# Column-tiled attention outputs, a new plan and another hand-over in a three-stage kernel

## The chip, the cores and the metric

One core of one Trainium2 chip runs the whole program; there is no communication. The metric is the device time of one execution in microseconds (us). Engines are named as the profile names them: PE is TensorE (PEld its weight loads), DVE is VectorE, ACT is ScalarE, POOL is GpSimd, SP is SyncE, whose queue issues nearly all DMAs. Each engine works through its own instructions in order, and waits on the others by semaphores.

## The reference

Three layers, one after the other, all in float32. `layout` lays the inputs out on the host before the kernel is launched, as it did before.

```python
# 1. attention with a complex decay: B, H, S, D = 2, 8, 768, 48
scale = np.minimum(mag, 0.999) / (mag + 1e-06)        # mag = |a_re + i a_im|
for t in range(S):
    S_re, S_im = a*S (complex) + k[t] v[t]^T           # state: D x D per head
    y[:, :, t] = q[t] @ S_re
# 2. mixture of experts on the 1536 x 384 rows: E = 8, F = 1024, capacity 384
e = argmax(x @ w_gate); pos = running count of e       # each row goes to one expert
y = relu(disp[e] @ w1[e]) @ w2[e];  out[i] = gate[i] * y[e, pos]
# 3. feed-forward, d_ff = 2048
h = x @ w_in
out = (max(h, 0) + alpha * min(h, 0)) @ w_out
```

## The kernel before

**Attention and routing.** The 2 x 768 positions are 12 tiles of 128 (tiles 0 to 5 are the first batch, 6 to 11 the second). The recurrence is done by chunks: for each tile `log_polar` and `turns` take logarithm and angle of the decay, `decay` and `turns` sum them along the tile by a product with a triangular matrix (`pl`, `pt`), `rotate` scales and turns k and q (`kk`, `qq`, 96 numbers a head: cosine and sine parts), and `attend` does the rest. In `attend`, per half of four heads: `tr` transposes kk and qq by PE (`pkT`, `pqT`) and evicts them to `kT`, `qT`; `scores` makes the 128 x 128 products `sc` and masks them to `pT`; `outs` adds `pT` times v and `qT` times the carried state `Z` into `y`; `state` makes the tile's addition `u` to the state. Two DVE operations then update `Z`. In `outs` (L614, L618) the stationary operand is `pT` or `qT` of a head, and 128 columns of v or Z stream through, 48 of which are the head's; the 80 others fall on columns that the next head's product writes again. `y` so has positions on partitions and heads along the row, and is copied to `x`.

`route` takes groups of tiles: it transposes `x` (`px`), evicts `xT`, multiplies with the gate weights (`lg`), picks the expert, counts positions, and POOL scatters the rows of `x` to a buffer `xs_d` in HBM by an indirect DMA. That buffer, and parts of `ys_d` and `gs_d`, are cleared first by `clear` from a zeroed tile.

The order of all this is made by `Plan`: every step is entered with an engine, a cost and a rank, and `order` lists them by a greedy simulation; `emit` then ties the instructions of each engine in that order. Tables at the top of the file (GROUPS, RANK, SQUARE, EVICT, TURN) say how tiles are grouped for the two activation tables, which step goes first, and which engine takes the squares of `log_polar`, the evictions of `kT` and `qT`, and the rounding in `turns`. `whole` and `preload` load the first experts' weights during attention: float32 weights are split into a high part `wh` (ACT) and a low part `wl` (DVE) of type fp32r (L889, L893).

**Experts.** `first_expert` builds the input of expert 0 without waiting for the last scatter. `ffn` then runs 8 experts over 256 rows: per step `ft` nine products into `hp` (three weight/input pairs for each of three 128-row blocks), ACT and DVE make `gh` and `gl`, and `second` adds six products into two `y` tiles. Hooks in each step convert the next weights (`unit`, L288 to L294), gather the next expert's rows and transpose them (`split_rows`). `first_chunk` prepares the input of the third layer; it reads the scattered gates back from `gs_d` into `gsl`, and `first_chunk_rows` adds the rows of other experts.

**Feed-forward.** `ffn` three times over 512 rows and 16 steps; at each end four `y` tiles are evicted to `o` and stored.

Of the kernel before, what the change touches and what calls it, by code (L numbers as in the profile page):

```python
# [21 lines left out]
P = 128  # L22
HD = 48
NH = 8
DM = NH * HD
VW = DM - HD + P
# [11 lines left out]
C_TRI, C_TRIP, C_ONE, C_LAST, C_STRI, C_COL = (i * P for i in range(6))  # L38
C_IOT = C_COL + 2
C_TWIN = C_IOT + GT * NE  # L40
GROUPS = [[0], [1], [2, 3], [4, 5], [6, 7], [8, 9], [10, 11]]
# [6 lines left out]
SQUARE = 'AAAAAAAAAAAA'  # L48
EVICT = 'AAAA'
DOUBLE = (('AAA', 'GGG'),) * NTL  # L50
TURN = 'AV' * 6
ABS = 'V' * NTL
C_ACT, C_BIAS, C_TT, C_STT, C_PS, C_WIDE, C_SQ = 0.415, 0.51, 0.47, 0.5, 0.47, 0.87, 0.79
# [3 lines left out]
RANK = {'L': -4.0, 'T': -3.5, 'D': -2.0, 'R': -1.5, 'E': -0.5, 'A': 0.0, 'O': 0.5}  # L57
# [8 lines left out]
HK1 = 9  # L66


class Plan:
# [9 lines left out]
    def op(self, engine, cost, fn, use=(), put=(), new=(), after=(), lag=None, port=False):  # L79
# [19 lines left out]
        self.ops.append(dict(engine=engine, cost=cost, fn=fn, deps=deps, new=list(new), lag=lag, rank=self.rank, port=port))  # L99
        return n  # L100

    def order(self):
# [9 lines left out]
        start, done = [None] * n, [None] * n  # L112
        free = {}
# [9 lines left out]
        while ready:  # L123
            best = []
            for i in ready:
# [17 lines left out]
                ((t, i) for t, i in best if ops[i]["engine"] == engine and t <= first + SLACK), key=lambda x: (-ops[x[1]]["rank"], rest[x[1]], -x[1])  # L143
            )
            o = ops[i]
            start[i] = t
            done[i] = t + o["cost"] + o["lag"]
            free[o["engine"]] = t + o["cost"]
            if o["port"]:
                free["port"] = t + o["cost"]  # L150
# [20 lines left out]
def const_array():  # L171
# [5 lines left out]
    for c in range(2):  # L177
# [6 lines left out]
        [tri, tri / (2 * math.pi), one, last, tri - np.eye(P), cq, ck, io, twin, np.eye(P), np.tile(np.arange(SLOTS), (P, 1))],  # L184
# [6 lines left out]
def tile_kernel(  # L191
# [114 lines left out]
    wg = acp.tile([P, KC, NE], F32, name="wg")  # L306
# [20 lines left out]
    for t in vt:  # L327
        G.memset(t[:, DM:VW], 0.0)
    Zt = [acp.tile([96, VW], F32, name=f"Z{i}") for i in range(B)]
    for t in Zt:  # L330
        G.memset(t[:, DM:VW], 0.0)
        G.memset(t[:, 0:DM], 0.0)
# [34 lines left out]
    def load(g, names, cost=0.6):  # L367
        for i in groups[g]:
            for nm in names:
                src = {"ar": a_re, "ai": a_im, "q": q, "k": k, "v": v}[nm]  # L370

                def fn(i=i, nm=nm, src=src):
                    if nm == "v":
                        dst = tl[f"v{i}"] = vt[i % 6]
                        dst = dst[:, 0:DM]
                    else:
                        dst = buf(raw, nm, f"{nm}{i}", [P, DM], RAW[nm])
# [59 lines left out]
    def decay(i):  # L437
# [3 lines left out]
        def pl():  # L441
# [3 lines left out]
               use=[f"l{i}", "cst"], put=[p], new=[("pc", p)])  # L445
# [114 lines left out]
    def attend(i):  # L560
# [6 lines left out]
        def y():  # L567
            return psum("y", f"y{i}", [P, 512])
# [726 lines left out]
```

## Time and profile before

| | |
|---|---|
| median of 3 runs | 561.19 us (559.08 to 561.61) |
| the profiled execution | 555.74 us, of which the span of its instructions 554.0 us |
| mean granted TensorE clock | 0.983 |
| busy: PE, PEld | 508.6 us (92%), 466.2 us (84%) |
| busy: DVE, ACT, POOL | 336.1 us (61%), 321.6 us (58%), 71.7 us (13%) |
| DMA | 71.04 MB, mean 128 GB/s |

The profile is of one execution. Busy times are shares of the whole span, over stages that have different limits, so they have to be taken stage by stage. From 0 to about 182 us the core does attention and routing, to about 343 us the eight experts, to about 546 us the feed-forward layer; the rest is the last store. A matmul of float32 operands appears as two instructions (two passes), one of fp32r operands as one.

### The profile page before, as it was taken

The page shows a single profiled execution, that of the slowest core. Times are in us where ns is not written, and L with a number is a line of the kernel's source. Part 1 is how long each engine was busy: PE and PEld are TensorE (multiplying, and loading weights), DVE is VectorE, ACT ScalarE, POOL GpSimd, SP SyncE. Part 2 cuts the span into 40 slices and gives each one's busy share as a digit, 9 for nine tenths or more (in the row PEclk, how much of TensorE's full clock was granted, in tenths as well). Part 3 has the DMA queues.
Part 4 walks back from the last instruction along what each step waited for, and adds up shares of the span by engine and source line. Part 5 has one row for each costly group of instructions (what it writes and reads, how often), then busy time and mean ns, then how long its engine had stood idle before and what let it go on. Part 6 is the DMA issues. An engine that isn't in the chain of part 4 may idle for free.

```text
span 554.0 us, 8596 instructions
## 1 busy us (share of the span) xinstructions
PE 508.6 (92%) x3270; PEld 466.2 (84%) x3270; DVE 336.1 (61%) x617; ACT 321.6 (58%) x601; POOL 71.7 (13%) x83
## 2 busy tenths in 40 slices
PE   1677999999998969999999998999999999999994
PEld 0466798888997958999999986988999989999993
DVE  2555889997663536676658969797933433333431
ACT  6589999995643346665656425464644534443432
POOL 2203126160512400000000020202000000000000
PEclk9978999999999989999999999999999999999998
DMA  8897534320001557788886466354101000100001
GB/s 270 291 397 253 147 101 157 116 87 0 30 12 47 114 173 246 230 249 264 268 304 188 143 200 205 105 160 135 54 0 58 1 0 1 43 15 1 1 0 63
DMA packets 37411, 71.04 MB, mean 128 GB/s; under 512 B 4105, under 2 KB 30098, under 8 KB 36594
## 3 DMA queue, kind: packets, MB, share of 16 engines
q1 hardware_dynamic: 35570, 65.30, 36.5%
q0 software_dynamic: 1792, 5.12, 2.8%
q8 instruction: 27, 0.44, 0.4%
q14 instruction: 22, 0.18, 0.1%
HBM read 55.84 MB, written 14.56 MB: 127 GB/s over the span
## 4 chain that ended last, share of the span: by engine, by line
PE 71%; DVE 10%; DMA 8%; ACT 6%; issue 2%; POOL 1%; SPq 0%; POOLq 0%; DVEq 0%; ACTq 0%
PE hp L1033 26%; PE y L1023 26%; PE y L614 3%; PE sc L599 3%; PE y L618 2%; PE u L631 2%; DMA gs_d<-gate,sidx 2%; PE pqT L580 1%; DMA sw<-in_moe_w_out 1%; DMA st<-in_moe_w 1%; DVE wl L294 1%; PE pt L492 1%; PE pt L1005 1%; DMA cst<-in_consts 1%; PE pkT L580 1%
## 5 line engine op out<-in xcount | busy, mean ns | idle before, releaser
L1023 PE MATMUL y<-wh,gh 128*128 128x384 f32 x320 | 109.6, 343 | 3.8 <-ACT gh L1041 3.8
L1033 PE MATMUL hp<-xl,wh 128*128 128x256 f32 (+1 forms) x336 | 111.0, 330 | 2.1 <-DVE xl L1008 1.0
L1033 PE MATMUL hp<-xh,wh 128*128 128x256 f32 (+1 forms) x336 | 111.5, 332 | 1.2 <-ACT xh L1007 1.0
L1033 PE MATMUL hp<-xh,wl 128*128 128x256 f32 (+1 forms) x336 | 110.8, 330 | 0.0
L1023 PE MATMUL y<-wl,gh 128*128 128x384 f32 x320 | 108.0, 337 | 0.0
L1023 PE MATMUL y<-wh,gl 128*128 128x384 f32 x320 | 89.3, 339 | 0.3 <-DVE gl L1042 0.2
L294 DVE TENSOR_TENSOR wl<-st,wh 128x768 fp32r<-128x768 f32 (+1 forms) x63 | 67.5, 1071 | 32.8 <-ACT wh L293 31.6
L293 ACT ACTIVATE wh<-st 128x768 fp32r<-128x768 f32 (+1 forms) x63 | 59.0, 936 | 28.8 <-DMA st<-in_moe_w 20.6
L1048 DVE SCALAR_TENSOR_TENSOR gn<-gn,nalp,gp 128x512 f32<-128x512 f32 x48 | 36.0, 749 | 62.5 <-ACT gp L1047 62.5
L1046 ACT ACTIVATE gn<-hp 128x512 f32<-128x512 f32 x48 | 28.7, 598 | 71.2 <-PE hp L1033 60.4
L1033 PEld LDWEIGHTS hp<-xl,wh 128*128 128x128 f32 x336 | 63.5, 189 | 7.6 <-DVE xl L1008 1.2
L1033 PEld LDWEIGHTS hp<-xh,wh 128*128 128x128 f32 x336 | 63.5, 189 | 7.1 <-ACT xh L1007 1.3
L1033 PEld LDWEIGHTS hp<-xh,wl 128*128 128x128 f32 x336 | 63.6, 189 | 5.0
L1023 PEld LDWEIGHTS y<-wh,gh 128*128 128x128 f32 x320 | 60.4, 189 | 5.6 <-ACT gh L1041 4.2
L1023 PEld LDWEIGHTS y<-wl,gh 128*128 128x128 f32 x320 | 60.6, 189 | 1.3
L1023 PEld LDWEIGHTS y<-wh,gl 128*128 128x128 f32 x320 | 57.0, 189 | 1.4 <-DVE gl L1042 0.9
L1050 DVE TENSOR_TENSOR gl<-gn,gh 128x512 fp32r<-128x512 f32 x48 | 33.2, 691 | 29.5 <-ACT gh L1049 29.5
L1041 ACT ACTIVATE gh<-hp 128x256 fp32r<-128x256 f32 x64 | 24.5, 383 | 44.0 <-PE hp L1033 39.6
L390 POOL TENSOR_TENSOR ai<-ai 128x384 f32<-128x384 f32 x36 | 34.9, 969 | 75.7 <-ACT ai L447 73.8
L1049 ACT ACTIVATE gh<-gn 128x512 fp32r<-128x512 f32 x48 | 30.2, 629 | 22.0 <-DVE gn L1048 21.9
L614 PE MATMUL y<-vt,pT 128*128 128x128 f32 x192 | 36.8, 284 | 2.3 <-DVE pT L605 2.2
L1042 DVE SCALAR_TENSOR_TENSOR gl<-hp,gh 128x256 fp32r<-128x256 f32 x64 | 26.7, 421 | 12.0 <-ACT gh L1041 11.8
(166 smaller groups left out, 810.8 us busy)
## 6 DMA issues: line engine op xcount, KB each, us to landing
st<-in_moe_w SPq DMA_DIRECT2D x24, 512.0 KB, 4.5
st<-in_moe_w SPq DMA_DIRECT2D x32, 384.0 KB, 3.9
sw<-in_moe_w_in SPq DMA_DIRECT2D x6, 1024.0 KB, 5.0
sw<-in_moe_w_out SPq DMA_DIRECT2D x8, 768.0 KB, 4.3
xs_d<-zero SPq DMA_DIRECT2D x1, 4608.0 KB, 15.6
ys_d<-o SPq DMA_DIRECT2D x16, 192.0 KB, 4.0
rows<-xs_d SPq DMA_DIRECT2D x14, 192.0 KB, 4.7
ar<-in_a_re SPq DMA_DIRECT2D x12, 192.0 KB, 3.5
```

What stands on the lines that cost most here:

```text
L293: follow(A(out=wh[:, js], in_=st, func=ACTF.Copy), behind, "A")
L294: ins = eng[j].tensor_tensor(out=wl[:, js], in0=st, in1=wh[:, js].bitcast(F32), op=ALU.subtract)
L390: (V if e == "V" else G).tensor_tensor(out=t, in0=t, in1=t, op=ALU.mult)
L614: T.matmul(out=y()[:, o:o + P], lhsT=tl[f"pT{i}{hh}"][:, h, :], rhs=tl[vk][:, o:o + P], start=True, stop=(c == 0))
L1023: T.matmul(out=ys[t], lhsT=a[:, sl], rhs=b[:, f, :], start=(ft == 0 and m == 0), stop=(ft == nf - 1 and m == 2))
L1033: ins = T.matmul(out=hp, lhsT=a[:, c, fs], rhs=b[:, c, :], start=(n == 0), stop=(n == 3 * KC - 1))
L1041: last["A"] = A(out=gh, in_=hp, func=ACTF.Relu)
L1042: last["V"] = V.scalar_tensor_tensor(out=gl, in0=hp, scalar=0.0, in1=gh.bitcast(F32), op0=ALU.max, op1=ALU.subtract)
L1046: A(out=gn, in_=hp, func=ACTF.Relu, scale=-1.0)
L1048: V.scalar_tensor_tensor(out=gn, in0=gn, scalar=nalp[:, ft:ft + 1], in1=gp, op0=ALU.mult, op1=ALU.add)
L1049: last["A"] = A(out=gh, in_=gn, func=ACTF.Copy)
L1050: last["V"] = V.tensor_tensor(out=gl, in0=gn, in1=gh.bitcast(F32), op=ALU.subtract)
```

## The change

`outs` swaps its operands: v and Z (padded to 64 columns a head, HW = 64) are stationary, 64 columns wide, and `pT` or `qT` streams through. The output of a head is transposed, 64 partitions by 128 positions, and two heads share a 128-partition block of `y`, one in the lower and one in the upper 64 columns of the array. `y` is then already what `route` needs as `xT` (with padded gate weights, four blocks of 128 in place of three); `back` and `rows` turn it back to rows `x` for the scatter. `state` streams 64 columns in place of 96. There is one `Z` for both batches, and the first tile's update is one operation.

The plan gets other groups and ranks; the squares of `log_polar`, all roundings of `turns` and one of four evictions move to DVE; `setup` gets a late rank; `xs_d` is cleared in four pieces later on, `ys_d` and `gs_d` after the first routing. `keep_warm` puts products without use (13 in all) ahead of products for which the plan sees a gap. In the experts, `behind_weights` puts gathers and the load of `gsl` behind the weight loads on SP, step 0 takes the low-part inputs last, half of `first_chunk_rows` moves to the last step, and the last evictions of the feed-forward layer alternate between DVE and ACT with four buffers.

```diff
+HW = 64
-VW = DM - HD + P
+VW = NH * HW
-GROUPS = [[0], [1], [2, 3], [4, 5], [6, 7], [8, 9], [10, 11]]
+GROUPS = [[0], [1, 2], [3, 4], [5, 6], [7, 8], [9, 10], [11]]
-SQUARE = 'AAAAAAAAAAAA'
-EVICT = 'AAAA'
-TURN = 'AV' * 6
+SQUARE = 'V' * NTL
+EVICT = 'AAAV'
+TURN = 'V' * NTL
-RANK = {'L': -4.0, 'T': -3.5, 'D': -2.0, 'R': -1.5, 'E': -0.5, 'A': 0.0, 'O': 0.5}
+RANK = {'L': -6, 'T': -2.5, 'D': -2.2, 'R': -1.3, 'E': -2.1, 'A': -0.3, 'O': 1}
...
         def outs(hh):
             def products():
-                for h in range(4):
-                    o = (4 * hh + h) * HD
-                    T.matmul(
-                        out=y()[:, o:o + P], lhsT=tl[f"pT{i}{hh}"][:, h, :], rhs=tl[vk][:, o:o + P], start=True, stop=(c == 0)
-                    )
-                    if c:
-                        T.matmul(
-                            out=y()[:, o:o + P], lhsT=tl[f"qT{i}{hh}"][:, h, :], rhs=Z[:, o:o + P], start=False, stop=True
-                        )
+                for j in range(2):
+                    for w, (src, dst) in enumerate(((tl[vk], f"pT{i}{hh}"), (Z, f"qT{i}{hh}"))[:2 if c else 1]):
+                        for m in range(2):
+                            h = 2 * j + m
+                            o = (4 * hh + h) * HW
+                            T.matmul(
+                                out=y()[m * HW:(m + 1) * HW, 2 * hh + j, :], lhsT=src[:, o:o + HW], rhs=tl[dst][:, h, :],
+                                start=(w == 0), stop=(w == 1 or c == 0),
+                            )
...
         def out():
-            xt[i] = xpool.tile([P, DM], F32, tag="x", name="x", bufs=6)
-            A(out=xt[i], in_=y()[:, 0:DM], func=ACTF.Copy)
+            A(out=buf(wk, "xT", xk, [P, H // 2, P], GT), in_=y(), func=ACTF.Copy)
+        def back():
+            pt = psum("tr", p, [P, H // 2, P])
+            for j in range(H // 2):
+                T.transpose(pt[:, j, :], tl[xk][:, j, :], ident)
+        def rows():
...
-            plan.op("S", 18.0, clear, use=["ar6", "k4"], put=["zeroed"], lag=2.2)
+        if g in CLEAR:
+            plan.rank = CLEAR_RANK
+            for n in range(4):
+                plan.op("S", 3.6, lambda n=n: clear(n), use=[CLEAR[g]], put=["zeroed"], lag=2.2)
...
+    def keep_warm(where, n):
+        for _ in range(n):
+            T.matmul(out=where(), lhsT=tri[:, 0:where().shape[0]], rhs=tri, start=True, stop=True)
...
-            for c in range(KC):
-                for a, b in ((uh, xh), (uh, xl), (ul, xh)):
+            terms = ((uh, xh), (ul, xh), (uh, xl))
+            if ft:
+                order = [(c, a, b) for c in range(KC) for a, b in terms]
+            else:
+                order = [(c, a, b) for c in range(KC) for a, b in terms[:2]] + [(c, *terms[2]) for c in range(KC)]
...
-            o = fp.tile([P, DM], F32, tag="o", name="o", bufs=3)
-            A(out=o, in_=ys[t], func=ACTF.Copy)
+            last_ones = len(ends) > 1
+            o = fp.tile([P, DM], F32, tag="rows" if last_ones else "o", name="o", bufs=4 if last_ones else OB)
+            if ends[t % len(ends)] == "A":
+                A(out=o, in_=ys[t], func=ACTF.Copy)
+            else:
+                V.tensor_copy(out=o, in_=ys[t])
...
+    def behind_weights(ins):
+        tc.add_manual_dep(ins.ins, wloads[max(wloads)].ins.name, NOSYNC, reason="weights are needed sooner")
...
+        if e == NE - 1:
+            hooks[FT - 1].append(lambda behind: first_chunk_rows(behind, range(CHT // 2, CHT)))
```

What the plan makes of it shows in the order of the engines' instructions. On PE, before, the outputs of tile 1 (`y`, from the second tile's `pT` and `qT`) stand after its first scores; the next rows repeat the last two for the other heads:

```order
L599 MATMUL sc_514<-qT_508,kT_442 128x128 x4
L580 MATMUL pqT_523<-ident,qq_409 96x128 x4
L690 MATMUL px_535<-ident,x 128x128 x3
L614 MATMUL y_543<-vt_114,pT_530 128x128
L618 MATMUL y_543<-Z_125,qT_508 128x128
```

The same place in the change, tile 1 again (`px` is now the turning back of the transposed output):

```order
L607 MATMUL sc_545<-qT_538,kT_520 128x128 x4
L587 MATMUL pkT_556<-ident,kk_502 96x128 x4
L626 MATMUL y_564<-pT_553,vt_114 64x128 x2
L626 MATMUL y_564<-qT_515,Z 64x128 x2
L626 MATMUL y_564<-pT_553,vt_114 64x128 x2
L626 MATMUL y_564<-qT_515,Z 64x128 x2
L587 MATMUL pkT_579<-ident,kk_502 96x128 x4
```

Both halves of the scores now stand ahead of the first outputs, and two products with the same kind of operand follow each other. On DVE, before, the low parts of the first weights (`wl` from `st`) stand among the steps of the first batch (`t_654` belongs to tile 6, `f_694` to tile 5, the mask `pT_703` to tile 2):

```order
L893 TENSOR_TENSOR wl_133<-st_506,wh_132 128x1024
L409 TENSOR_TENSOR t_654<-t_654,ai_269 128x384
L509 TENSOR_SCALAR r_678<-pt_652 128x384
L893 TENSOR_TENSOR wl_133<-st_541,wh_132 128x1024
L514 SCALAR_TENSOR_TENSOR f_694<-r_678,pt_652 128x384
L605 TENSOR_TENSOR pT_703<-sc_671,cst 128x512
```

In the change they stand among tile 8's masks (`pT_1569`, `pT_1612`), beside an eviction that DVE now does (`qT`):

```order
L594 TENSOR_SCALAR qT_1552<-pqT_1533 96x512
L486 COPY ezs<-pz_1521 96x8
L921 TENSOR_TENSOR wl_123<-st_1040,wh_122 128x1024
L613 TENSOR_TENSOR pT_1569<-sc_1546,cst 128x512
L921 TENSOR_TENSOR wl_123<-st_1061,wh_122 128x1024
L542 TENSOR_SCALAR cs_1584<-f_1426 128x8x48
```

Of the seven conversions, one stands between tiles 5 and 6 and six stand from tile 8 on. On SP, at the hand-over to the experts, before (`rows` are gathered inputs of experts 1 and 2, `st` weight pieces, `gsl` the gates read back):

```order
L1071 DMA rows<-xs_d 128x384 x4
L288 DMA st_2207<-in_moe_w 128x2x384
L1149 DMA gsl<-gs_d 128x2x1
L288 DMA st_2231<-in_moe_w 128x2x384
L288 DMA st_2267<-in_moe_w 128x2x384
L288 DMA st_2291<-in_moe_w 128x2x384
```

and in the change:

```order
L1131 DMA rows<-xs_d 128x384 x2
L300 DMA st_2228<-in_moe_w 128x2x384
L300 DMA st_2252<-in_moe_w 128x2x384
L300 DMA st_2288<-in_moe_w 128x2x384
L300 DMA st_2312<-in_moe_w 128x2x384
L300 DMA st_2338<-in_moe_w 128x1024
```

The load of `gsl` has left this place (it stands in the last expert), and two gathers stand behind six weight pieces.

## Rows read from the trace of the kernel before

**Rows 1.** Busy time by stretch: engines, then granted clock, DMA share, GB/s.

```profile
0.00:30.00 30.00, 10.73 (x43) 6.61 (x43) 12.02 (x28) 19.52 (x38) 7.26 (x21) 1.00 0.88 290
30.00:120.00 90.00, 84.04 (x635) 73.87 (x636) 73.41 (x165) 86.52 (x175) 27.60 (x27) 0.94 0.54 179
120.00:176.00 56.00, 54.81 (x483) 51.17 (x481) 35.16 (x86) 30.22 (x57) 15.31 (x17) 1.00 0.09 30
176.00:210.00 34.00, 26.14 (x166) 23.63 (x166) 16.64 (x46) 14.31 (x25) 7.80 (x7) 0.95 0.52 143
210.00:343.00 133.00, 130.35 (x918) 127.30 (x916) 98.24 (x150) 75.09 (x136) 4.07 (x4) 1.00 0.70 226
343.00:554.00 211.00, 202.48 (x1031) 183.59 (x1031) 100.59 (x144) 95.94 (x173) 9.62 (x8) 0.99 0.14 46
```

**Rows 2.** Costliest groups, the two of `outs`: shapes, count, busy us, mean ns.

```profile
L614 PE MATMUL y<-vt,pT 128*128 128x128 f32 x192 | 36.8, 284 | 2.3 <-DVE pT L605 2.2
...
L618 PE MATMUL y<-Z,qT 96*128 96x128 f32 x160 | 31.5, 278 | 0.0
```

**Rows 3.** Timeline, PE, 146 to 151 us: start, us, engine, line, operation.

```profile
146.33 0.84 PE L631 MATMUL u<-vt,kk 128*96 128x96 f32 x8
147.10 0.37 PE L466 MATMUL pz<-ident,ar 32*96 32x32 f32 x4
147.41 0.64 PE L580 MATMUL pkT<-ident,kk 128*96 128x128 f32 x4
...
150.81 0.39 PE L614 MATMUL y<-vt,pT 128*128 128x128 f32 x2
151.04 0.39 PE L618 MATMUL y<-Z,qT 96*128 96x128 f32 x2
```

**Rows 4.** L614 alone, 120 to 176 us: PE, PEld.

```profile
120.00:176.00 56.00, 16.87 (x89) 13.07 (x88) 1.00 0.09 30
```

**Rows 5.** L618 alone, 120 to 176 us: PE, PEld.

```profile
120.00:176.00 56.00, 15.45 (x80) 12.11 (x80) 1.00 0.09 30
```

**Rows 6.** L414 alone (the squares), 30 to 120 us: ACT.

```profile
30.00:120.00 90.00, 4.19 (x8) 0.94 0.54 179
```

**Rows 7.** L585 alone (evictions of kT and qT), two stretches: ACT.

```profile
30.00:120.00 90.00, 17.26 (x30) 0.94 0.54 179
120.00:176.00 56.00, 10.21 (x18) 1.00 0.09 30
```

**Rows 8.** L893 alone (low parts of weights), 30 to 120 us: DVE.

```profile
30.00:120.00 90.00, 7.43 (x7) 0.94 0.54 179
```

**Rows 9.** Timeline, DVE, 99 to 107 us, back to back.

```profile
99.62 0.55 DVE L664 TENSOR_TENSOR Z<-Z,ezs 96x384 f32<-96x384 f32 x1
100.09 0.61 DVE L550 SCALAR_TENSOR_TENSOR ai<-k,cst,ai 128x384 f32<-128x384 f32 x1
...
105.45 0.69 DVE L605 TENSOR_TENSOR pT<-sc,cst 128x512 f32<-128x512 f32 x1
106.05 0.95 DVE L555 TENSOR_TENSOR kk<-ai,cs 128x768 f32<-128x768 f32 x1
```

**Rows 10.** Timeline, ACT at 28 us; in brackets the idle time before.

```profile
27.76 0.52 ACT L414 ACTIVATE w<-t 128x384 f32<-128x384 f32 x1 [2.88 <-DVE t L409]
```

**Rows 11.** Timeline of the hand-over, 196 to 210 us, PE, ACT and SP.

```profile
196.77 0.84 ACT L293 ACTIVATE wh<-st 128x768 fp32r<-128x768 f32 x1 [6.67 <-DMA st<-in_moe_w]
...
196.94 0.37 SPq L1149 DMA_DIRECT2D gsl<-gs_d  x1
...
197.94 0.69 PE L1023 MATMUL y<-wh,gh 128*128 128x384 f32 x1 [3.51 <-ACT gh L1041]
...
200.85 0.84 ACT L293 ACTIVATE wh<-st 128x768 fp32r<-128x768 f32 x1 [2.96 <-DMA st<-in_moe_w]
...
209.44 0.39 PE L1033 MATMUL hp<-xl,wh 128*128 128x256 f32 x1 [1.02 <-DVE xl L1008]
```

**Rows 12.** Timeline, PE in the last expert.

```profile
329.59 0.71 PE L1188 MATMUL pt<-ident,rows 128*128 128x128 f32 x4 [1.04 <-DVE rows L1185]
```

**Rows 13.** Timeline, ACT at the end.

```profile
548.26 0.49 ACT L1062 ACTIVATE o<-y 128x384 f32<-128x384 f32 x1 [1.54 <-DMA out<-o]
```

More of the change, by code (lines that the diff above doesn't have):

```diff
@@ L77, in __init__, with op @@
         self.writer, self.readers, self.tagged, self.users = {}, {}, {}, {}
-    def op(self, engine, cost, fn, use=(), put=(), new=(), after=(), lag=None, port=False):
+    def op(self, engine, cost, fn, use=(), put=(), new=(), after=(), lag=None, port=False, fill=None):
         n = len(self.ops)
@@ L326, in tile_kernel @@
     vt = [acp.tile([P, VW], F32, name=f"vt{i}") for i in range(6)]
[L327 to L332, printed above, removed]
+    Z = acp.tile([96, VW], F32, name="Z")
+    G.memset(Z, 0.0)
     tl = {}
@@ L964, in emit @@
                 engines[ins.engine] = ins.name
+    def keep_warm(where, n):
+        for _ in range(n):
+            T.matmul(out=where(), lhsT=tri[:, 0:where().shape[0]], rhs=tri, start=True, stop=True)
+    idle_from = 0.0
     for n in plan.order():
-        emit(plan.ops[n]["fn"])
+        o = plan.ops[n]
+        if o["engine"] == "T":
+            gap = plan.start[n] - max(idle_from, WARM_FROM)
+            idle_from = plan.start[n] + o["cost"]
+            if o["fill"] is not None and gap > FILL_MIN:
+                emit(lambda: keep_warm(o["fill"], min(int(FILL * gap / C_FILL), FILL_MAX)))
+        emit(o["fn"])
     first_expert()
@@ L1030, in ffn @@
             n = 0
-            for c in range(KC):
-                for a, b in ((uh, xh), (uh, xl), (ul, xh)):
-                    ins = T.matmul(out=hp, lhsT=a[:, c, fs], rhs=b[:, c, :], start=(n == 0), stop=(n == 3 * KC - 1))
-                    if n == 0 and last["hp"] is not None:
-                        tc.add_manual_dep(ins.ins, last["hp"].ins.name, NOSYNC, reason="one block after the other")
-                    n += 1
+            terms = ((uh, xh), (ul, xh), (uh, xl))
[3 more added lines that the diff above has]
+                order = [(c, a, b) for c in range(KC) for a, b in terms[:2]] + [(c, *terms[2]) for c in range(KC)]
+            for c, a, b in order:
+                ins = T.matmul(out=hp, lhsT=a[:, c, fs], rhs=b[:, c, :], start=(n == 0), stop=(n == 3 * KC - 1))
+                follow(ins, {"h": last["h0"]} if ft == 0 and n else None, "h")
+                last["h0"] = ins
+                if n == 0 and last["hp"] is not None:
+                    tc.add_manual_dep(ins.ins, last["hp"].ins.name, NOSYNC, reason="one block after the other")
+                n += 1
             last["hp"] = last["h"] = ins
@@ L1180, in first_chunk, with first_chunk_rows @@
         chunk0.update(xh=xh, xl=xl, gsl=gsl, os=os, pts=pts, rows=got)
-    def first_chunk_rows(behind):
-        for j, rows in enumerate(chunk0["rows"]):
+    def first_chunk_rows(behind, some):
+        for j in some:
+            rows = chunk0["rows"][j]
             follow(
@@ L1228, in turned @@
             else:
-                first_chunk_rows(behind)
+                first_chunk_rows(behind, range(CHT // 2))
         def store(t, o, e=e):
```

163 lines of the change are left out of this document (99 added, 64 removed).

## The prediction

> **What bounds the kernel now.** I read the busy time by stretch first, then the costliest groups, then the timeline at the places that the change touches. The stretches [rows 1] show different limits. From 30 to 120 us ACT is busy 86.5 of 90 us (96%); PE with 84.0 and DVE with 73.4 (82%) are not far from it. From 120 to 176 us PE is busy 54.8 of 56 us while DVE has 35.2 and ACT 30.2: PE ends this stretch. From 176 to 210 us, the end of routing and the first expert, PE has only 26.1 of 34 us, so something late holds it. From 210 to 343 and from 343 us on PE is full (130.4 of 133 and 202.5 of 211); only the seams can give anything there. The groups [rows 2] name the two products of `outs`: 192 + 160 = 352 passes. Their mean of 280 ns is mostly latency; the price is the step from one to the next, 0.23 us for two passes (150.81 to 151.04, rows 3), 0.11 us each, so 39 us of PE's time.
>
> **The outputs.** `outs` keeps its 352 passes and the 128 columns that stream in each. New is that two neighbours use different 64-column halves of the array. If these run beside each other, a pair costs what one costs now, and 352 x 0.11 / 2 = 19.4 us go; if not, nothing goes. No row shows two halves at work, so these are the ends. I take the pair: what else could hold it, the weight loads, already runs beside products (from 120 to 176 us 51.2 us of loads inside PE's 54.8, rows 1). In the stretch that PE ends stand 89 + 80 = 169 of the passes [rows 4, 5], worth 9.3 us; the other 183, worth 10.1, stand almost all from 30 to 120 us.
>
> The Trainium skill ("TensorE: Matmul & The Clock Gate", Part 3, on packing small matmuls) says that a weight load overlaps a running product only where their row groups differ. Two column halves share all rows, so by that rule this term would shrink to nothing, the first rival below; the trace agrees poorly, since loads that share all rows do overlap here.
>
> A change of shape of the array costs little by the trace: eight passes of `u` from 146.33, four of the 32-row `pz` from 147.10, and the next at 147.41 [rows 3], 0.08 to 0.10 us a pass with no gap to be seen. The Trainium skill ("TensorEngine Tiling (Array Packing)", Key Properties) says that a change of tiling mode drains the engine; the row shows no such wait, and the sum would grow only if the 48 changes of `outs` were of another kind.
>
> **What the transposed output adds.** Per tile one transpose and two passes of `lg` more (four blocks for three): 36 passes x 0.11 = 4.0 us of PE, 2.3 us for seven tiles before 120 us and 1.7 for five after. The eviction of `y` is wider, about 0.1 us of ACT a tile. `state` streams 64 columns for 96: at 0.096 us a pass (rows 3) at most a third of 160 passes, 5 us, may go, at least nothing, and I take nothing, since the weight load stays as wide. The 13 products without use are 26 x 0.11 = 2.9 us where they stand in the way; they may give back clock, as the granted clock was 0.94 from 30 to 120 us (full is 2.4 GHz, the other level 1.2), some 5 us of PE's time where PE is not what ends. I take 0 of -5 to +3.
>
> **What moves from ACT to DVE.** Twelve squares, eight of them from 30 to 120 us [rows 6]; a quarter of the evictions, so 7.5 of 30 before 120 us and 4.5 of 18 after [rows 7]; six roundings, some four before. DVE's price is its step back to back [rows 9]: 0.47 us for 384 elements (99.62 to 100.09), 0.60 for 512 out of PSUM (105.45 to 106.05). The weight conversions, seven before 120 us with 7.4 us [rows 8], stand from tile 8 on but for one: 6.4 us go from the first stretch to the second, and ACT's halves with them.
>
> First stretch, DVE: 73.4 + 8 x 0.47 + 4 x 0.47 + 7.5 x 0.60 - 6.4 = 77.1 us. PE: 84.0 - 10.1 + 2.3 = 76.2. ACT: 86.5 - 4.2 - 17.3 / 4 - 4 x 0.47 + 0.7 = 76.8 even with its part of the conversions left in, and that goes too. So DVE is late next, with PE at its heels. At the 96% that the bound engine reaches now the stretch would take 80.4 us; with two engines that close I take 93%, 83 us: -7. Second stretch, DVE: 35.2 + 6.4 + 4.5 x 0.60 + 2 x 0.47 = 45.2; PE: 54.8 - 9.3 + 1.7 = 47.2, at its present 98% 48 us; I take 50, as DVE has come near: -6. At the start ACT waits 2.9 us for DVE [rows 10], which does `setup` just before; that is now late in DVE's order, while a third tile's logarithms are added to the start: between 0 and -3, I take -1.5. Attention ends 14.5 us earlier.
>
> **Zeros, order of loads.** The 4.6 MB of `xs_d` are cleared behind the inputs of the next tiles. No wait of ACT on DMA stands between 30 and 120 us that this could remove (it is 96% busy), and the scatters need the zeros only after the first routing. I cost it at nothing; the cover is that POOL is busy 27.6 of 90 us. If the zeros land late, the squares of `ai` behind the first scatter on POOL wait as long, and DVE's scaling of k behind them. The late zeros of `ys_d` stand on SP among weight loads of attention, whose conversions have moved back as well.
>
> **The hand-over.** ACT waits 6.7 us for a weight piece until 196.77, and PE 3.5 us behind it; `gsl`, which needs the scattered gates, is issued at 196.94, three pieces queue behind it, and ACT waits another 3.0 us until 200.85 [rows 11]. Without `gsl` there the first wait stays (it was issued ahead of `gsl`), the second goes, and with it most of the lag of the next expert, whose first products wait to 209.44. I take -4: the 3.0 us and the 1.0 us of `xl`, which step 0 now takes last; between -1 and -8, if two gathers less in front also bring the first piece sooner.
>
> **Seams and end.** In the last expert PE waits 1.0 us for `rows` [rows 12], half of which now come later: -1. At the end the fourth eviction waits 1.5 us for a buffer to be stored [rows 13]; with four buffers it does not: -1.5.
>
> The sum: -14.5 - 4 - 1 - 1.5 = -21. The profiled execution took 555.74 us, 1% less than the median of the runs shown, so it would become 534.7; against the median of 561.19 I forecast 540.
>
> **The rivals.** (1) The halves of the array run one after the other. PE: 84.0 + 2.3 from 30 to 120 us, no gain at 96% (90); 54.8 + 1.7 = 56.5 in the second stretch, +1.7. Attention gains -1.5 + 1.7 = 0, and 6.5 us of seams remain: 555. For it: nothing in the trace shows two halves at work. Against it: the loads that overlap. (2) Slower: DVE becomes the bound and cannot be filled. It takes work that PE waits for (evictions of `qT`) in a queue where masks, squares and conversions that wait on ACT, POOL or DMA stand in front, so that PE and DVE wait for one another by turns. After 30 us DVE would have 108.6 + 13.3 = 122 us of work (73.4 + 35.2, and 8 x 0.47 for squares, 5 x 0.47 for roundings, 12 x 0.60 for evictions). The seams give 6.5 us, so the kernel is slower than before if these 122 us take more than 146 + 6.5 us, a share below 80%; at 75% they take 163, and the kernel 561 + 17 - 6.5 = 571. For it: 82% is all that DVE reaches now from 30 to 120 us. Against it: there ACT was full, and is no longer. (3) The plan does not fit and half of the attention gain is lost, stretches of 87 and 53 us: 547. (4) The second stretch and the hand-over come out at their better ends, and `state` and the clock give some: 530.
>
> **How the numbers follow.** The forecast has 45%, (3) 18% and (4) 12%; with these two its own range is 530 to 548. Rival (1), the halves in a row, has 14%, rival (2) 11%. The range that leaves out at most two in ten goes from 529 to 555. Within 0.5% (2.8 us, about what a measurement of this kernel can tell from no change) lies a part of rival 1 with some drain and the mild part of rival 2: 8%. Slower by more: 9%. Faster by more: 83%.
>
> **What would show it.** Right: starts of `outs` passes 0.055 us apart on average; the second stretch ended near 161 us, not 176; DVE above 90% from 30 to 110 us and ACT near 85%; no DMA wait of ACT after the first weight piece in expert 0; the last eviction without a wait. Wrong: passes still 0.11 us apart (rival 1); DVE and PE both under 85% with waits on each other, most of all PE on `qT` or `pT` (rival 2); POOL's first scatter waiting for the zeros.

## The result and the profile after

The changed kernel takes 542.6 us (median; 541.57 to 544.29) against 560.56 us (559.08 to 561.61): a ratio of 0.969 with a 95% interval of 0.966 to 0.972, 18 us faster. The forecast was 540 us, the range 529 to 555. The two profiled executions lie closer together, 555.74 and 544.29 us. So the kernel before was also run again beside the experiments (`c_before`, below), and its second trace, of an ordinary execution, is the measure in this table. Its times are differences between the starts of single passes in the traces, in us:

| stretch, and what ends it | before [rows 1 to 13] | before, second trace | after | after less second | predicted |
|---|---|---|---|---|---|
| attention: last pass of `outs` | 174.6 | 176.6 | 161.5 | -15.1 | -14.5 |
| end of routing: first `hp` of expert 0 | 7.3 | 8.6 | 10.4 | +1.8 | 0 |
| expert 0: first `hp` of expert 1 | 26.1 | 26.1 | 24.6 | -1.5 | -4 |
| experts 1 to 7: first `hp` of the feed-forward layer | 134.3 | 134.9 | 135.2 | +0.3 | -1 |
| feed-forward layer: last product | 203.3 | 205.0 | 202.6 | -2.5 | 0 |
| last eviction and store | 8.4 | 8.3 | 7.9 | -0.4 | -1.5 |
| span | 554.0 | 559.6 | 542.2 | -17.4 | -21 |

In a second trace of the changed kernel (`c_after`, below) the six stretches take 161.8, 10.5, 23.2, 133.4, 203.0 and 7.5 us, so single stretches differ by up to 2 us from one execution to the next.

The first view is the busy time by stretch of the kernel after, the answer to [rows 1], with the same columns and the borders where its stages end.

```profile
0.00:30.00 30.00, 16.88 (x83) 13.13 (x84) 15.85 (x35) 21.23 (x41) 3.98 (x10) 0.89 0.75 238
30.00:120.00 90.00, 84.84 (x710) 69.84 (x708) 80.17 (x184) 75.02 (x148) 29.05 (x30) 0.92 0.54 178
120.00:162.00 42.00, 41.51 (x425) 36.18 (x424) 37.12 (x89) 28.23 (x51) 16.18 (x14) 1.00 0.26 85
162.00:176.00 14.00, 10.34 (x64) 9.64 (x65) 5.81 (x30) 5.34 (x9) 7.11 (x8) 0.76 0.34 62
176.00:197.00 21.00, 17.19 (x107) 16.42 (x106) 11.00 (x16) 9.77 (x18) 1.63 (x2) 0.92 0.74 179
197.00:330.00 133.00, 129.66 (x915) 127.69 (x914) 98.20 (x151) 73.91 (x134) 5.33 (x4) 0.99 0.71 230
330.00:542.20 212.20, 204.42 (x1037) 184.62 (x1035) 104.65 (x151) 95.00 (x169) 8.87 (x8) 0.99 0.14 46
```

From 30 to 120 us ACT has gone from 96% to 83% and DVE from 82% to 89%; PE, with 94%, is the fullest. From 120 us PE is full as before, and attention ends 13 us sooner. Behind it stands the emptiest row but the first, from 162 to 176 us: PE has 10.3 of 14 us at a granted clock of 0.76. Next the outputs of the last tile, PE's timeline, which answers to the last two of [rows 3].

```profile
159.81 0.44 PE L626 MATMUL y<-pT,vt 128*64 128x128 f32 x4
160.08 0.40 PE L626 MATMUL y<-qT,Z 96*64 96x128 f32 x4
160.32 0.39 PE L626 MATMUL y<-pT,vt 128*64 128x128 f32 x4
160.54 0.39 PE L626 MATMUL y<-qT,Z 96*64 96x128 f32 x4
```

Four passes now take the 0.22 us that two took, 0.055 us a pass. The starts of the single passes show how: neighbours, which by the program's order are a pass of the lower and one of the upper half, start 7 to 10 ns apart, and the next two 0.10 us later. Then the end of routing, timeline of POOL, DVE and PE.

```profile
162.87 1.18 POOL L807 DMA_DIRECT2D rows<-xs_d  x2 [3.46 <-issue]
164.33 0.99 POOL L836 TENSOR_TENSOR al<-x,ah 128x384 fp32r<-128x384 f32 x1 [0.28 <-ACT ah L835]
...
164.41 0.93 DVE L733 SCALAR_TENSOR_TENSOR cand<-cand,cst 128x16 f32<-128x16 f32 x1
...
166.03 0.49 PE L823 MATMUL pb<-ident,rows 128*128 128x128 f32 x2 [1.96 <-DMA rows<-xs_d]
```

PE waits 2.0 us for scattered rows that in the trace before had landed long before their turn, and a small step of DVE in the choice of the expert takes 0.93 us for 0.17. The hand-over, timeline of SP, ACT and PE, answers to [rows 11].

```profile
177.12 14.31 SPq L300 DMA_DIRECT2D st<-in_moe_w  x6
...
186.03 0.84 ACT L305 ACTIVATE wh<-st 128x768 fp32r<-128x768 f32 x1 [5.93 <-DMA st<-in_moe_w]
...
187.19 0.44 PE L1070 MATMUL y<-wh,gh 128*128 128x384 f32 x1 [2.70 <-ACT gh L1094]
...
188.03 0.84 ACT L305 ACTIVATE wh<-st 128x768 fp32r<-128x768 f32 x1 [0.89 <-DMA st<-in_moe_w]
...
197.96 0.62 PE L1084 MATMUL hp<-xl,wh 128*128 128x256 f32 x3 [0.42 <-DVE xl L1055]
```

The first wait is 5.9 us for 6.7, the second 0.9 for 3.0, the one for `xl` 0.4 for 1.0. The seam into the feed-forward layer, DVE and PE, has a wait that [rows 12] don't show:

```profile
326.56 0.56 DVE L289 TENSOR_SCALAR st<-sw 128x768 uint32<-128x768 uint32 x1 [0.66 <-DMA sw<-in_moe_w_out]
327.04 0.61 DVE L1263 SCALAR_TENSOR_TENSOR yl<-y,gsl,yh 128x384 fp32r<-128x384 f32 x1
...
327.71 1.65 PE L1268 MATMUL pt<-os,yl 128*128 128x512 f32 x3 [1.57 <-DVE yl L1263]
```

DVE waits for a weight piece with `yl` queued behind it, and PE waits for `yl`. At the end, the answer to [rows 13], ACT's two last evictions stand back to back:

```profile
534.34 0.87 ACT L1117 ACTIVATE o<-y 128x384 f32<-128x384 f32 x2 [3.32 <-PE y L1070]
```

### The profile page after: what moved, and what is told of

Its sections match the earlier page's. It is cut to its first block, busy times and chain, and to the rows that moved or that the text cites. A ratio compares the mean times of both kernels' runs of the same rounds, so it can differ in the third digit from the quotient of the medians.

```text
span 542.2 us, 8708 instructions
## 1 busy us (share of the span) xinstructions
PE 504.8 (93%) x3332; PEld 457.5 (84%) x3332; DVE 352.8 (65%) x651; ACT 308.5 (57%) x565; POOL 72.2 (13%) x74
## 4 chain that ended last, share of the span: by engine, by line
PE 78%; DMA 7%; DVE 7%; ACT 4%; issue 2%; SPq 0%; ACTq 0%; DVEq 0%
PE hp L1084 30%; PE y L1070 28%; PE y L626 3%; DMA st<-in_moe_w 2%; PE sc L607 2%; PE pt L499 2%; PE u L640 2%; PE pt L502 1%; PE pqT L587 1%; PE pkT L587 1%; PE pl L451 1%; PE pt L1052 1%; DMA rows<-ys_d,eidx 1%; DMA cst<-in_consts 1%; ACT ar L395 1%
## 5 line engine op out<-in xcount | busy, mean ns | idle before, releaser
L1084 PE MATMUL hp<-xl,wh 128*128 128x256 f32 (+1 forms) x336 | 107.9, 332 | 0.4 <-DVE xl L1055 0.4
L1094 ACT ACTIVATE gh<-hp 128x256 fp32r<-128x256 f32 x64 | 24.6, 384 | 48.7 <-PE hp L1084 48.5
L397 POOL TENSOR_TENSOR ai<-ai 128x384 f32<-128x384 f32 x36 | 36.3, 1008 | 84.7 <-ACT ai L454 82.8
L1100 ACT ACTIVATE gp<-hp 128x512 f32<-128x512 f32 x48 | 28.4, 592 | 0.0
```

What stands on the lines that cost most here:

```text
L397: (V if e == "V" else G).tensor_tensor(out=t, in0=t, in1=t, op=ALU.mult)
L1084: ins = T.matmul(out=hp, lhsT=a[:, c, fs], rhs=b[:, c, :], start=(n == 0), stop=(n == 3 * KC - 1))
L1094: last["A"] = A(out=gh, in_=hp, func=ACTF.Relu)
L1100: A(out=gp, in_=hp, func=ACTF.Relu)
```

## The experiments

Each is set against the runs of the kernel before on its own chip, as a ratio with its 95% interval; the changed kernel has 0.9689 (0.9662 to 0.9715), and 0.9716 (0.9676 to 0.9756) in its second set, `c_after`. 1% is 5.6 us.

**c_before: the kernel before once more.** No edit.

> The kernel before, unchanged. The two profiled executions differ by 11.8 us (span 554.0 and 542.2), the medians by 18.0 (560.56 and 542.6). Theory: the profiled execution of before, 555.74 us at a mean clock of 0.983, was an uncommonly quick one, and its other executions have a lower mean clock. Then the runs here lie at 559 to 562 us with a clock of about 0.975, ratio 1.00 +- 0.003, and a second trace shows the missing 5 us as low granted clock behind PE's waits before 210 us. Rival: runs of the same clock differ by 5 us for another reason (DMA), then the clock here is 0.983 again in a run of 560 us.

559.79 us (557.14 to 561.87), ratio 1.0009 (0.9976 to 1.0042), clock of the profiled run 0.974. The first profiled execution was a quick one. Of the 5.6 us between the two spans, 2.0 lie in attention (granted clock 0.91 for 0.94 from 30 to 120 us), 1.3 in the end of routing, 1.9 in one wait of PE's weight loads in the feed-forward layer, which the first trace doesn't have:

```profile
382.30 0.19 PEld L1033 LDWEIGHTS hp<-xh,wl 128*128 128x128 f32 x1 [1.89 <-DVE wl L294]
```

The granted clock also falls in the end of routing here, where it is 1.00 in the first trace. So the theory holds in part: some of it is clock, some a late weight conversion.

**e_same_half: one half of the array first.**

```diff
-                for j in range(2):
-                    for w, (src, dst) in enumerate(...):
-                        for m in range(2):
+                for m in range(2):
+                    for j in range(2):
+                        for w, (src, dst) in enumerate(...):
```

> The changed kernel; only the order of the eight products of each outputs step differs: first the four that use the lower 64 columns of the array, then the four that use the upper ones, so neighbours nearly always use the same half. Theory of the prediction (two halves run beside each other): neighbours can't pair any more, passes go back from 0.055 to 0.11 us apart, PE gets 352 x 0.055 = 19.4 us more, 9 of them in the stretch that PE ends: 552 to 562 us. Rival: a pass costs what its weight load costs, which with 64 columns is half of that with 128, whichever half: passes stay 0.055 us apart, 541 to 545 us.

549.11 us (546.66 to 550.19), ratio 0.9814 (0.9768 to 0.9859): 1.0 to 1.3% more than the two sets of the changed kernel, 5 to 7 us, between the two expectations. PE's timeline of the last tile says why:

```profile
167.34 0.43 PE L626 MATMUL y<-qT,Z 96*64 96x128 f32 x2 [0.40 <-DVE Z L689]
167.61 0.44 PE L626 MATMUL y<-pT,vt 128*64 128x128 f32 x4
...
169.10 0.38 PE L626 MATMUL y<-pT,vt 128*64 128x128 f32 x2
169.32 0.38 PE L626 MATMUL y<-qT,Z 96*64 96x128 f32 x2
```

Passes with no partner (x2) are 0.11 us apart, so a narrower load alone buys nothing. But in the middle four of one kind still stand together (x4), though in the program no two products with the same kind of operand are neighbours: products of the upper half run beside those of the lower that stand ahead of them. The trace does not print the half of a pass, so this is read from the kinds of operand alone. Half of the pairing survives: 0.083 us a pass on average against 0.054 (mean distance of starts, gaps above 0.2 us left out).

**e_wide: no pairing possible.** The order of the run before, and:

```diff
-    out=y()[m * HW:(m + 1) * HW, 2 * hh + j, :], lhsT=src[:, o:o + HW],
+    out=y()[m * HW:P, 2 * hh + j, :], lhsT=src[:, o:o + P - m * HW],
```

> As the run with one half first, but the products of the lower half take 128 stationary columns instead of 64 (the 64 too many fall on the upper half, which the upper head's products write again afterwards). The stream of 128 columns and the number of passes stay. If a pass costs its weight load, 176 of 352 passes go from 0.055 to 0.11 us: 9.7 us of PE's time, at least the 4 to 5 us of them in the stretch that PE ends, 546 to 553 us. If instead halves run beside each other or the stream sets the price, the time is that of the run with one half first, within 1.5 us.

559.94 us (553.38 to 561.4), ratio 0.9998 (0.996 to 1.0036). PE's timeline, the outputs of one tile:

```profile
166.66 0.39 PE L626 MATMUL y<-pT,vt 128*128 128x128 f32 x2
166.88 0.39 PE L626 MATMUL y<-qT,Z 96*128 96x128 f32 x2
...
167.69 0.38 PE L626 MATMUL y<-pT,vt 128*64 128x128 f32 x2
167.91 0.38 PE L626 MATMUL y<-qT,Z 96*64 96x128 f32 x2
```

Passes of 128 and of 64 columns alike are 0.11 us apart. Both the load-width theory (546 to 553 us) and the stream theory fall; only two halves at work explain the three runs. Without the pairs the whole change is worth nothing by this run: attention ends at 181.7 us, 5 later than in `c_before`, and the stages behind it make up for that. Some of the 5 us may be this run's own. Where its passes change between 128 and 64 columns they start 0.20 us apart, so its mean distance (gaps above 0.3 us left out) is 0.127 us, against 0.118 to 0.121 in the two traces of the kernel before: 2 to 3 us of PE's time over 352 passes.

**e_act_work: squares, evictions and roundings back on ACT.**

```diff
-EVICT = 'AAAV'
+EVICT = 'AAAA'
-SQUARE = 'V' * NTL
+SQUARE = 'A' * NTL
-TURN = 'V' * NTL
+TURN = 'AV' * 6
```

> The changed kernel with the twelve squares, the quarter of the evictions and the six roundings back on ACT as before, planned anew. Theory of the prediction: ACT ended the stretch from 30 to 120 us before, and would again: its 75.0 us there grow by 8 x 0.52 + 7.5 x 0.58 + 4 x 0.47 = 10.4 us to 85.4, which at 96% is the old stretch, so +5 to +8: 548 to 551 us. Rival: the narrower outputs and the later weight conversions were the gain, and ACT has room for this: 541 to 545 us.

553.09 us (548.14 to 553.53), ratio 0.9863 (0.9806 to 0.9921): by the ratios 8 to 10 us more than the changed kernel, more than the +5 to +8 expected. Busy time by stretch, to be held against the second row of the kernel after:

```profile
30.00:120.00 90.00, 80.25 (x691) 66.26 (x690) 68.31 (x163) 81.77 (x164) 27.49 (x29) 0.96 0.55 185
```

ACT is the fullest again (91%, PE 89%), PE and DVE get less done in the same time, and attention ends at 171.7 us. Pairing without the move keeps 6 to 8 of the 18 us (medians 558.65 and 553.09; 1.4% by the ratio), the move without pairing none (`e_wide`): together they are worth more than one by one. The busy shares fit an engine that is not relieved and sets the pace, ACT here and PE in `e_wide` (86.2 of 90 us, 96%).

**e_handover: the old hand-over.**

```diff
 def behind_weights(ins):
-    tc.add_manual_dep(ins.ins, wloads[max(wloads)].ins.name, NOSYNC, ...)
+    pass
...
-            if ft:
+            if True:
                 order = [(c, a, b) for c in range(KC) for a, b in terms]
```

> The changed kernel with the hand-over of before: the gathers and the load of gsl stand on SP where the program reaches them, ahead of weight pieces, and step 0 takes its nine products in the old order. Theory of the prediction: +4 us (between 1 and 8), with a second DMA wait of ACT of 2 to 3 us in expert 0 and a wait of PE for xl of 1 us at expert 1: 545 to 548 us. Rival: the first weight piece of the hand-over is late in either order and everything behind it follows from that one, +0 to +1.5 us: 542 to 544 us.

544.36 us (544.2 to 546.58) against 542.21 (541.39 to 544.87) for `c_after` in the same set, ratio 0.9752 (0.9713 to 0.9791): about 2 us, half of the prediction's 4. The intervals overlap, but five of the six runs of `c_after` lie below all six here. In the two traces expert 0 takes 26.0 us for 23.2, but the end of routing 9.0 for 10.5. ACT's timeline has the second wait again:

```profile
186.48 0.84 ACT L305 ACTIVATE wh<-st 128x768 fp32r<-128x768 f32 x1 [7.14 <-DMA st<-in_moe_w]
190.10 0.84 ACT L305 ACTIVATE wh<-st 128x768 fp32r<-128x768 f32 x1 [2.51 <-DMA st<-in_moe_w]
```

(1.0 us in `c_after`), and PE's waits for `gh` and for `xl` are 4.0 and 0.9 us, for 2.7 and 0.3 in `c_after`.

**e_rows_last: the wait at 166 us taken off PE's path.** The loop over `rows0` in `first_expert` moves behind each block of products with `ah` and `al`.

```diff
-        for c in range(KC):
-            for j in range(SLOTS // P):
-                ins = add(c, rows0[j], ident, slice(j * P, (j + 1) * P))
...
                 for a, b in parts:
                     add(c, a, b)
+            for c in range(KC)[cs]:
+                for j in range(SLOTS // P):
+                    add(c, rows0[j], ident, slice(j * P, (j + 1) * P), ...)
```

> The changed kernel; the six products that add the gathered rows to the input of expert 0 stand behind those of the last two tiles' rows, not ahead of the last routing counts. In the trace of the changed kernel PE waits 1.96 us for these rows at 166.03 us, the routing counts stand behind it on PE, and the granted clock is 0.76 from 162 to 176 us. Theory: this wait holds up the routing and with it everything behind; without it expert 0 starts 1.5 to 2.5 us sooner: 539 to 541.5 us. Rival: the first weight piece of the hand-over ends later anyway, PE waits longer for it, +-0.5 us.

542.99 us (541.17 to 544.2), ratio 0.9719 (0.968 to 0.9759): nothing. My theory fell. PE's wait for the rows is gone, but PE now waits there for DVE's choice of the expert, and expert 0 starts at 172.1 us as before:

```profile
164.74 0.94 DVE L733 SCALAR_TENSOR_TENSOR cand<-cand,cst 128x16 f32<-128x16 f32 x1
...
166.71 0.17 PE L749 MATMUL pp<-ocb,onesb 128*128 128x16 bf16 x1 [2.32 <-DVE ocb L741]
```

That step of DVE ends when POOL's `al` ends (164.66 + 0.99 us). It takes 0.17 us in `c_before`, where `al` ran 2 us earlier: `x` was then evicted ahead of `xT`, now it is turned back from it.

**e_early_conv: the weights that lie there converted ahead of expert 0.**

```diff
+    for _ in range(KC):
+        work(None, 4)
...
         for ft in range(FT):
-            hooks[ft].append(lambda behind, e=e: work(behind, 2 * e + 4))
+            if e or ft >= KC:
+                hooks[ft].append(lambda behind, e=e: work(behind, 2 * e + 4))
```

> The changed kernel; the three conversions of the weights of expert 1 that lie in their buffers since 162 us stand ahead of the first step of expert 0 on ACT and DVE, not in its steps 0 to 2 (the later pieces keep their places). In the trace of the changed kernel the next three pieces can't be loaded until these buffers are free (issue at 177.12 us), and ACT waits 5.93 us for the first of them at 186.03, PE 2.70 us behind it. Theory: the loads are issued 1.5 to 3 us sooner and these waits shrink by as much, against a delay of 1 to 2 us of the first gh: -0.5 to -2 us, 540.5 to 542 us. Rival: three conversions in a row ahead of gh cost PE 2 to 3 us at expert 0, +0 to +2 us.

540.03 us (537.33 to 542.56), ratio 0.9659 (0.9613 to 0.9705): 2.2 us less by the medians, though the intervals overlap. ACT's waits, timeline:

```profile
182.46 0.84 ACT L305 ACTIVATE wh<-st 128x768 fp32r<-128x768 f32 x1 [1.98 <-DMA st<-in_moe_w]
183.98 0.85 ACT L305 ACTIVATE wh<-st 128x768 fp32r<-128x768 f32 x1 [0.41 <-DMA st<-in_moe_w]
```

The loads are issued from 175.49 us, 1.6 us sooner than in the changed kernel, and the first wait ends 3.6 us sooner (182.46 us for 186.03): part of the delay was in buffers that were not free. Why the load also takes 2 us less is not shown.

**e_yl: the last weight pieces behind the seam.**

```diff
+            if e < NE - 1 or ft < 2:
                 hooks[ft].append(lambda behind, e=e: work(behind, 2 * e + 4))
...
         if c == 0:
+            for ft in range(2):
+                hooks[ft].append(lambda behind: work(behind, GATE - 1))
```

> The changed kernel; the last two of the four pieces of the first output weights of the feed-forward layer are converted in its steps 0 and 1 instead of steps 2 and 3 of the last expert. In all traces with the changed tail DVE waits for the load of the last piece with yl queued behind it, and PE waits 1.5 to 1.6 us for yl (0 to 0.3 us before). Theory: this wait was made by the change of the last expert's order, and goes here: -1.5 us, or -2.5 where the granted clock falls behind it, 539.5 to 541 us. Rival: the rows of the last step or the first xh end later anyway, +-0.5 us.

543.42 us (540.36 to 545.78), ratio 0.9751 (0.972 to 0.9783): no gain. The wait for `yl` is gone, and the feed-forward layer starts 27.4 us after expert 7 for 28.5 in `c_after`. But the layer itself is 1.8 us longer (204.8 for 203.0), and PE's weight loads wait there for a later piece, which the moved pieces have held up by my reading,

```profile
363.68 0.19 PEld L1084 LDWEIGHTS hp<-xh,wl 128*128 128x128 f32 x1 [1.36 <-DVE wl L306]
```

the same kind of wait as in `c_before`. The gain was given back within 38 us.

**e_no_fill: without the 13 products that have no use.**

```diff
-FILL, FILL_MIN, FILL_MAX, C_FILL = 0.6, 0.5, 14, 0.23
+FILL, FILL_MIN, FILL_MAX, C_FILL = 0.6, 0.5, 0, 0.23
```

> The changed kernel without its 13 products without use. The prediction took 0 of a range from -5 (clock given back) to +3 (in the way). If they only stand in the way: -0.5 to -3 us, 539 to 541.7 us. If they hold the granted clock up: +1 to +5 us, and the clock of 30 to 120 us is below the 0.92 of the changed kernel. Neither: within 0.5 us of 542.2.

537.58 us (535.92 to 539.45), ratio 0.9645 (0.9613 to 0.9677): 4.6 us less than `c_after` by the medians, 2.5 to 4 us less by the ratios of the changed kernel's two sets. Those sets ran on other chips, and the intervals just overlap; but all six runs lie below all ten of the changed kernel (541.39 to 544.87). Apart from the 13 products every engine has the same instructions in the same order in the two traces. Busy time by stretch:

```profile
0.00:30.00 30.00, 14.99 (x64) 10.13 (x64) 17.15 (x37) 22.58 (x44) 5.15 (x11) 1.00 0.74 243
30.00:120.00 90.00, 84.92 (x745) 69.84 (x744) 83.14 (x189) 77.97 (x153) 30.09 (x32) 0.96 0.53 176
```

From 30 to 120 us the granted clock is 0.96 without them and 0.92 with them, not lower; with them it is 0.94 in `e_both`. The 1.00 of the first 30 us is no reading of a clock: PE's timeline below has four passes in 0.86 us until 24.93 us and in 0.43 us from 27.01 us on, so PE stood at the lower of its levels (1.2 GHz) until some 25 us. The column starts with the first change that the trace records, and counts what lies ahead as full. `c_after`, with a row of 0.89 there, reaches the shorter distance at some 24 us (25.11 to 25.54 for four passes), so the two hardly differ. The first product that is needed is late by the eight that stand in front, PE's timeline of `c_after`:

```profile
8.98 3.78 PE L1004 MATMUL pl<-cst 128*128 128x128 f32 x16 [8.98 <-DMA cst<-in_consts]
12.55 1.43 PE L451 MATMUL pl<-l,cst 128*128 128x384 f32 x2
...
25.11 0.60 PE L587 MATMUL pkT<-ident,kk 128*96 128x128 f32 x4
25.54 0.60 PE L587 MATMUL pqT<-ident,qq 128*96 128x128 f32 x4
```

and of `e_no_fill`:

```profile
9.99 1.65 PE L451 MATMUL pl<-l,cst 128*128 128x384 f32 x2 [9.99 <-DVE l L437]
...
24.07 1.06 PE L587 MATMUL pqT<-ident,qq 128*96 128x128 f32 x4
24.93 0.90 PE L640 MATMUL u<-vt,kk 128*96 128x64 f32 x8
...
27.01 0.60 PE L587 MATMUL pqT<-ident,qq 128*96 128x128 f32 x4
27.45 0.60 PE L587 MATMUL pkT<-ident,kk 128*96 128x128 f32 x4
```

Attention ends at 158.4 us for 161.8, and expert 0 starts 8.5 us later for 10.5, with no wait for the scattered rows. The products of `c_after` lag behind the same ones here by 2.6 us at the first `pl` and by 2.0 us from 50 to 100 us. Then the granted clock of `c_after` falls, busy time by stretch of `c_after` and, below, of `e_no_fill`,

```profile
100.00:110.00 10.00, 8.99 (x72) 7.48 (x71) 9.10 (x36) 8.25 (x16) 4.71 (x5) 0.80 0.25 79
...
100.00:110.00 10.00, 8.54 (x76) 6.93 (x75) 9.41 (x37) 8.95 (x16) 5.42 (x6) 1.00 0.24 79
```

and the lag grows to 4.6 us. `e_both`, `e_early_conv`, `e_ends` and `e_yl` have the 13 products and a granted clock of 1.00 from 100 to 120 us, so the products need not bring that fall. There the lag stays between 2.2 and 3.6 us from 50 to 150 us.

**e_ends: the old end.**

```diff
-        ffn(*xc, ..., hooks, ends="VA")
+        ffn(*xc, ..., hooks)
```

> The changed kernel with the old end: all four last evictions of a part on ACT, through three buffers. By the prediction the fourth waits 1.5 us for a store again: +1.5 us, 543.5 to 544 us. By the two traces, from the last product to the issue of the last store 3.5 us passed before and 2.75 us now: +0.8 us.

545.21 us (544.06 to 548.0), ratio 0.9793 (0.9758 to 0.9828): 3 us by the medians, some 4 by the ratio to `c_after`, at least twice the prediction's term. The eviction waits again,

```profile
535.79 0.49 ACT L1117 ACTIVATE o<-y 128x384 f32<-128x384 f32 x1 [1.95 <-DMA out<-o]
```

which makes 1.3 us from the last product to the end (8.8 for 7.5 in `c_after`), close to the prediction's 1.5. Another 1.1 us stand in the feed-forward layer (204.0 for 203.0). Its first two parts end in the same way, but the waits that `c_after` does not have stand 23 us ahead of the first of these ends (396.7 us), PE's weight loads:

```profile
371.69 0.65 PEld L1070 LDWEIGHTS y<-wh,gl 128*128 128x128 f32 x4 [0.33 <-DVE gl L1103]
...
373.28 0.19 PEld L1070 LDWEIGHTS y<-wh,gh 128*128 128x128 f32 x1 [0.77 <-ACT gh L1102]
```

From 344 us on, 15 us into the first part, the instructions of DVE and PE stand in another order than in `c_after`, so the edit changed more than the ends. The rest of the 3 to 4 us is not placed.

**e_both: the early conversions and the late pieces together.** Both edits.

> The changed kernel with the early conversions for expert 1 and the late pieces of the feed-forward weights together. If the two waits are independent, both gains add up: -2.2 and -1.5 us, 538 to 539.5 us, faster than the changed kernel. If experts 1 to 7 wait for weights at the rate of the loads, the first gain is given back before the last expert and only -1.5 us remain: 540 to 541 us.

539.99 us (535.27 to 541.96), ratio 0.9675 (0.9632 to 0.9717): the gain of the early conversions alone. The two do not add up, since the second gives its gain back here too (feed-forward layer 205.0 us). The fastest kernel of all is the one without the 13 products, 537.6 us; with the early conversions it was not run.

## Why the prediction was right, and where it was not

**Pairs of outputs: right in mechanism and size.** 0.11 to 0.055 us a pass, 19.4 us of PE's time, and 16 to 17 us of the kernel's (0.9998 less 0.9716 or 0.9689, `e_wide`), 2 to 3 of which may be that run's own. The first rival is refuted. It would have been worse than I gave it: not 555 us but no change. The Trainium skill ("TensorE: Matmul & The Clock Gate", Part 3, what overlaps and what doesn't) has a weight load overlap running products only where their row groups differ. Here two halves that share all rows start within 10 ns of each other, their weight loads too (160.541 and 160.548 us, beside passes that by the profile end at 160.70 and 160.71), so the trace disagrees with that sentence. The same list has matmuls start and end strictly in program order; `e_same_half` shows passes that by their operands are the upper half's overtaking the lower half's.

**ACT's work to DVE: right.** Undoing it costs 8 to 10 us. From 30 to 110 us DVE is busy 72.8 of 80 us (91%, "above 90%") and ACT 68.8 (86%, "near 85%"). But I named DVE late next with PE at its heels; with 94% it is PE. The second rival, DVE that can't be filled, didn't come.

**Attention as a whole: -15.1 for -14.5, by errors that cancel, which is luck.** The products without use were taken at 0 of -5 to +3; `e_no_fill` puts them at +2.5 to +4.6 in all, and at +3.4 in attention against `c_after` (161.8 less 158.4). The other traces with them end attention at 159.6 to 162.2 us, so +1.2 to +3.8; without them it would have gained 16 to 19 us. That is the step of attention that failed by most, near or beyond the end of its own bounds: I priced a pass at 0.11 us, but the sixteen of the first eight take 3.6 us (8.98 to 12.55), 0.22 each, the price at the lower level of the clock, and the first `pl` is 2.6 us later for them. A second term was put at nothing: the change of shape, which was read from `pz` as free. PE's timeline after, four passes and the change behind them:

```profile
153.09 0.39 PE L626 MATMUL y<-qT,Z 96*64 96x128 f32 x4
153.41 0.64 PE L587 MATMUL pqT<-ident,qq 128*96 128x128 f32 x4
```

They take 0.32 us where four passes inside a block take 0.22. Wherever no wait stands between, the step into a block of outputs and the step out of it take 0.18 to 0.20 us after and mostly 0.08 to 0.11 before, and the first pair takes 0.05 us more. With 21 blocks in the trace I estimate 4 to 5 us of PE's time, a quarter of what the pairs give. Where the errors of the other sign lie I can't say, since the two moves above can't be priced apart.

**What no term held: the end of routing, +1.8.** I followed attention to its last output and took what lies behind as fixed. A shorter attention leaves the scatters of tiles 8 and 9 less time ahead of their use (gather issued at 162.87, needed at 164), `al` now collides with the choice of the expert on DVE (0.8 us), and PE falls to the lower level of its clock: the twelve `pb` and `pa` products of `oh` start 0.21 us apart after (169.60 to 169.81), 0.12 before (180.61 to 180.73). `e_rows_last` shows that taking the first of these away alone moves nothing. The other traces say which of them counts. The slow step of DVE (0.94 us) stands in `e_wide` and `e_same_half` too, where the end of routing takes 7.7 us with the rows in time and a granted clock of 1.00, against 7.3 in the first trace of the kernel before, also at 1.00. With the rows in time and one fall of the clock it takes 8.4 and 8.5 us (`e_yl`, `e_no_fill`, 0.88 from 162 to 176 us), and 10.2 to 11.2 where PE waits or idles for about 2 us. So the collision alone adds little; most of the 1.8 us goes with the wait for the rows and the clock that falls behind it, and how much each of these two takes stays open.

**Hand-over: right in mechanism, half the size.** The first wait stays, as said; the second shrinks from 3.0 to 0.9 us, where none was forecast. The measured price is 2 us, not 4. That PE was held by the first wait and the second stood partly behind it is my reading; the end of routing, 1.5 us shorter in `e_handover`, hides part of the price (expert 0 alone is 2.8 us longer there). `e_early_conv` shows where a part of the first wait comes from.

**Seams.** The rows taken later gave what was said (0.8 us of wait for 1.0, and less behind it), but moved the last expert's steps against the weight conversions, and the wait for `yl` (0 to 0.3 us before, 1.6 after) took it back: the sum is +0.3, not -1, in the first trace. `c_after` has the same wait and takes 133.4 us there, -1.5. Between the two stands the clock: behind the wait it is granted at 0.57 from 327 to 331 us in the first trace, and 1.00 in the second. So the forecast of -1 is neither shown nor refuted. The end works as said and at the size said, 1.3 us for 1.5; the 3 to 4 us of `e_ends` hold 1.1 us that lie ahead of any end, and a rest that is not placed. Zeros and order of loads were costed at nothing; no wait for zeros stands in the trace, but they were not tried alone.

The total came out 2.6 us from the forecast, and that is partly luck, since errors of both signs are in it. By the last two columns of the table they are -0.6, +1.8, +2.5, +1.3, -2.5 and +1.1 us, together +3.6; and of the -2.5 in the feed-forward layer 1.9 are a wait that the kernel before has in one of its two traces only.

## What to carry to other kernels

Where two engines are both near full, price a relief of one by what the other then allows, and look for edits that are worth more together than alone. Follow a stage that gets shorter past its end: transfers that were hidden behind it (a scatter and its gather, buffers waiting to be freed) are the next wait. A product without use is not free where PE idles: what stands behind it in the queue is late. And hold a granted clock of 1.00 at the start of a trace against the distances of the passes before building on it.

## What was not expected of the hardware

Passes of one column half overtake earlier ones of the other half (`e_same_half`, rows x4, read from their operands), so PE does not always take its passes in the order in which they stand, and that order matters less for pairing than it seems.

A DVE step on 128x16 numbers, 0.17 us alone, took 0.93 us while POOL's 0.99 us `al` ran, and ended with it. The Trainium skill ("SBUF — State Buffer", SBUF: two separate sides) describes an exclusive lock between a DVE step with two SBUF inputs and a GpSimd step; the trace agrees.

Products without use did not raise the granted clock: 0.92 to 0.94 with them (`c_after`, `e_both`) and 0.96 without (`e_no_fill`, one trace) from 30 to 120 us, and PE first came to the distance of the higher level and stayed there at some 24 us (`c_after`) and 25 us (`e_no_fill`).
